# One scan and a long reciprocal per chunk, a shift in the weight merge, and a new order of the first 42 tasks, in a linear-attention and feed-forward kernel

## The chip, the cores and the metric

The kernel runs on one core of a Trainium2 chip. The metric is the device time of one execution in microseconds (us), the median of several runs; less is better. The engines are named as in the profile: PE is TensorE (matmuls), PEld its weight loads, DVE is VectorE, ACT is ScalarE, POOL is GpSimd, and SP is SyncE, which here only issues transfers (DMAs). Each engine works through its own list of instructions in order. SBUF is the working memory, PSUM the memory that PE writes to, in eight banks.

## The reference

The reference has two parts. The first is a linear attention over 768 positions for 4 batches and 8 heads of 48 dimensions, all in float32:

```python
for t in range(S):
    cur = einsum('bhd,bhe->bhde', u[None] * k_t, v_t)
    y[:, :, t] = einsum('bhd,bhde->bhe', r_t, state + cur)
    state = w_t[:, :, :, None] * state + einsum('bhd,bhe->bhde', k_t, v_t)
```

The decays w lie between 0.8 and 0.95. The second part takes the 3072 tokens of 384 values that come out of this: `h = x @ w_in` (384 to 2048), `g = h * sigmoid(1.702 h)`, `out = g @ w_out` (2048 to 384).

## The kernel before, in words

**Attention.** The positions are cut into chunks of 128; with 4 batches there are 24 chunks, six to a batch. Two heads share the partitions, so that a chunk is handled as four pairs of heads (NP = 4) on 112 partitions. For a chunk, DVE first makes running products of the decays with a scan along the free dimension, all four pairs in one instruction of 4 x 129 = 516 elements; a zero between the pairs starts each pair anew. Before, there are two scans: one backwards (line 288), which gives the products from each position to the end of the chunk (`li`) and at the pair's first place the product over the whole chunk (`total`); then a reciprocal of the four totals (line 291), which is written into the constant operand `d1f`; and a scan forwards that starts from it (line 293), giving `pm`. Then one multiplication (line 299) makes kq, that is k and r scaled by the two products. PE transposes kq (ps_t, 306), ACT copies the transposed half (kt, 308). The diagonal term with u comes from k times r (rku, 314), a small product on PE (ps_d, 326), a copy (s, 329) and a scaling of a masked identity by s (am): by eight ACT instructions for the chunks in `BY_ACT` (336), by two DVE instructions for the others (341). PE then makes the chunk's contribution to the state and the scores within the chunk (ps_u, 356 and 360). DVE multiplies the old state sf by `total` (366) and adds the contributions of the two halves (mid, 367, and the new sf, 370), and puts the scores into am (373). PE makes the output ps_y from am, v, qf, sf and mid (383, 396); a one-element copy (406) stands between two groups of these. At last `split` writes y as a high part in the format that PE takes (ACT, 230) and the rest as a low part (DVE, 231) into the tile x.

**Checks in the kernel.** The fast path is only right if no sum overflows. For this, ACT squares the tile of both products (`lp`) and kq and adds up (236); at the end a comparison over all these sums (571) decides whether a slow path is run.

**Feed-forward.** Weights arrive as 64-bit floats in 12 slices (`fetch`, tags f), six of w_in and six of w_out, through three buffers st. `convert` (tags w, four steps) turns a slice into a float32 and splits it: two ACT passes over the low and the high words (216, 217), two DVE merges (219, 222), the high part by ACT (224) and the low part by DVE (226). The tile x of a group of four chunks is 512 wide. A task is one of 16 column blocks of d_ff for one group; the first 20 tasks are half-width, each for two chunks of group 0. For a task PE makes ph (g, lines 438 to 440, nine matmuls), ACT makes gelu twice (h, 449 and 450), DVE the low part (gl, 452), and PE the second product po (y, 465 to 467, nine matmuls). Before the first product of a half group, a fill copies rows of x across partitions by six DMAs (425), of which SP and POOL issue three each.

**What sets the order.** For tasks from 42 on, a table of steps (`PARTS`) gives each piece of a chunk a place relative to its task. For the first 42 tasks the order is written out by hand in `RAMP`: each word is a piece (l a load, a the next step of a chunk, w of a weight slice, m of the sums, f, g, h, y, x as above, u and M small loads), and d with a number puts that many matmuls on constant data ahead of the next use of a PSUM bank. Every engine gets its instructions in this order.

Of the kernel before, what the change touches and what calls it, by code (L numbers as in the profile page):

```python
# [94 lines left out]
def rwkv_ffn_kernel(ctx: ExitStack, tc, wkr, vp, vrk, ub, w_in, w_out, masks, vt, uc, out):  # L95
# [133 lines left out]
    def split(hi, lo, f):  # L229
        A.copy(hi, f)  # L230
        V.tensor_tensor(lo, f, hi.bitcast(F32), op=ALU.subtract)
# [453 lines left out]
```

## Time and profile before

| What | Value |
|---|---|
| Median of 3 runs | 512.39 us (511.4 to 512.84) |
| Profiled execution | 512.25 us |
| Its span in the profile | 510.5 us |
| PE busy | 490.8 us, 5065 matmuls |
| DVE busy | 296.8 us, 507 instructions |
| ACT busy | 249.8 us, 532 instructions |
| DMA | 45.94 MB, mean 90 GB/s |

The span is the time between the first and the last instruction of the profiled execution. [...] In the rows of groups, the name left of the arrow is what is written and right of it what is read, then come shapes (partitions x elements) and count, then busy time in us, the mean of one in ns, and the idle time ahead of them with what ended it. In the rows of a timeline, the first number is the start and the second the length, in us.

### The profile page before, as it was taken

Reading aid. Unit: us, or ns where it says so; the run is one execution under the profiler, and the core shown is the slowest. Engines: PE = TensorE matmul, PEld = TensorE weight load, DVE = VectorE, ACT = ScalarE, POOL = GpSimd, SP = SyncE. Lnnn points to the kernel's source line nnn. Section 1 sums busy time; section 2 is a strip of 40 time slices with the busy share of each in tenths; the row PEclk is TensorE's granted clock in tenths of the full one; section 3 lists DMA queues with packets and bytes.
Section 4 is the critical chain, followed back from the end, with each engine's and each line's share of the span. In section 5 each row is a group of like instructions: output and inputs, shape, how many; then the busy total and the mean of one; then the engine's idle time right before and its main releaser. Section 6 shows DMA issues by size and latency. Waiting matters only on the chain.

```text
span 510.5 us, 11971 instructions
## 1 busy us (share of the span) xinstructions
PE 490.8 (96%) x5065; PEld 407.7 (80%) x5065; DVE 296.8 (58%) x507; ACT 249.8 (49%) x532; POOL 13.7 (3%) x45
## 2 busy tenths in 40 slices
PE   7788999999999999999999999999999999999994
PEld 3567999987888888888888888888888878888883
DVE  8899999787777762656556555555655521111110
ACT  4887989856726453352542543452552432322221
POOL 2010100000100010000001000001000000000000
PEclk9998899999999999999999999999999999999999
DMA  8988665034641532042204062204040001100001
GB/s 211 261 251 233 195 185 158 17 88 133 173 125 31 172 82 60 1 157 63 79 2 121 5 193 83 68 1 125 16 142 1 1 1 31 63 0 2 0 2 68
DMA packets 26830, 45.94 MB, mean 90 GB/s; under 512 B 4096, under 2 KB 17856, under 8 KB 26768
## 3 DMA queue, kind: packets, MB, share of 16 engines
q1 hardware_dynamic: 25984, 43.52, 29.9%
q0 software_dynamic: 672, 1.18, 1.2%
q8 instruction: 42, 0.69, 0.6%
q10 hardware_dynamic: 112, 0.39, 0.2%
q14 instruction: 20, 0.16, 0.1%
HBM read 38.00 MB, written 4.72 MB: 84 GB/s over the span
## 4 chain that ended last, share of the span: by engine, by line
PE 89%; DMA 5%; DVE 3%; ACT 1%; issue 1%; SPq 0%; DVEq 0%; ACTq 0%
PE po L465 14%; PE ph L438 13%; PE po L466 13%; PE po L467 13%; PE ph L439 13%; PE ph L440 13%; DMA wkr_t<-in_wkr 3%; PE ps_y L396 3%; PE ps_y L383 3%; PE ps_u L360 2%; PE ps_u L356 2%; DMA st<-in_w_in 2%; PE ps_t L306 2%; PE ps_d L326 1%; DVE lp L288 0%
## 5 line engine op out<-in xcount | busy, mean ns | idle before, releaser
L452 DVE TENSOR_TENSOR gl<-gf,gh 128x512 fp32r<-128x512 f32 (+1 forms) x106 | 67.9, 641 | 156.6 <-ACT gf L450 155.4
L449 ACT ACTIVATE gh<-ph 128x512 fp32r<-128x512 f32 (+1 forms) x106 | 59.2, 558 | 197.5 <-PE ph L440 177.8
L438 PE MATMUL ph<-x,wih 128*128 128x512 f32 (+1 forms) x318 | 119.8, 377 | 1.4 <-DMA x<-x 1.4
L465 PE MATMUL po<-gh,woh 128*128 128x512 f32 (+1 forms) x318 | 120.6, 379 | 0.0
L466 PE MATMUL po<-gh,wol 128*128 128x512 f32 (+1 forms) x318 | 118.2, 372 | 0.0
L467 PE MATMUL po<-gl,woh 128*128 128x512 f32 (+1 forms) x318 | 118.2, 372 | 0.0
L440 PE MATMUL ph<-x,wil 128*128 128x512 f32 (+1 forms) x318 | 117.4, 369 | 0.0
L439 PE MATMUL ph<-x,wih 128*128 128x512 f32 (+1 forms) x318 | 117.4, 369 | 0.0
L438 PEld LDWEIGHTS ph<-x,wih 128*128 128x128 f32 x318 | 59.9, 188 | 12.2 <-ACT junk L236 1.9
L465 PEld LDWEIGHTS po<-gh,woh 128*128 128x128 f32 x318 | 60.5, 190 | 10.8
L467 PEld LDWEIGHTS po<-gl,woh 128*128 128x128 f32 x318 | 60.6, 190 | 10.5 <-DVE gl L452 0.2
L466 PEld LDWEIGHTS po<-gh,wol 128*128 128x128 f32 x318 | 60.6, 191 | 9.5
L440 PEld LDWEIGHTS ph<-x,wil 128*128 128x128 f32 x318 | 59.9, 188 | 10.3
L439 PEld LDWEIGHTS ph<-x,wih 128*128 128x128 f32 x318 | 60.0, 189 | 9.4
L450 ACT ACTIVATE gf<-ph 128x512 f32<-128x512 f32 (+1 forms) x106 | 58.8, 555 | 2.7 <-DVE gl L452 2.6
L236 ACT ACTIVATE junk<-lp 112x1032 bf16<-112x1032 f32 x24 | 25.6, 1066 | 12.6 <-DVE lp L293 12.6
L299 DVE TENSOR_TENSOR kq<-wkr_t,lp 112x1024 f32<-112x1024 f32 x24 | 29.3, 1222 | 2.6 <-PE ps_y L396 1.6
L288 DVE TENSOR_TENSOR_SCAN lp<-wkr_t,d1r 112x516 f32<-112x516 f32 x24 | 29.4, 1225 | 1.7 <-DMA wkr_t<-in_wkr 1.7
L293 DVE TENSOR_TENSOR_SCAN lp<-wkr_t,d1f 112x516 f32<-112x516 f32 x24 | 29.6, 1231 | 0.7
L396 PE MATMUL ps_y<-kq,mid 64*64 64x64 f32 (+3 forms) x384 | 24.6, 223 | 3.6 <-DVE mid L406 1.4
L236 ACT ACTIVATE junk<-kq 112x1024 bf16<-112x1024 f32 x24 | 25.4, 1059 | 0.2
L396 PEld LDWEIGHTS ps_y<-kq,mid 64*64 64x64 f32 (+3 forms) x384 | 19.6, 130 | 5.6 <-DVE mid L406 2.1
(76 smaller groups left out, 475.1 us busy)
## 6 DMA issues: line engine op xcount, KB each, us to landing
st<-in_w_out SPq DMA_DIRECT2D x6, 1024.0 KB, 7.5
rk_t<-in_vrk SPq DMA_DIRECT2D x16, 384.0 KB, 3.5
st<-in_w_in SPq DMA_DIRECT2D x6, 896.0 KB, 8.4
v_t<-in_vrk SPq DMA_DIRECT2D x24, 192.0 KB, 2.8
out_t<-ob SPq DMA_DIRECT2D x18, 256.0 KB, 2.5
wkr_t<-in_wkr SPq DMA_DIRECT2D x18, 192.0 KB, 2.6
wkr_t<-in_wkr SPq DMA_DIRECT2D x36, 96.0 KB, 2.3
wkr_t<-in_wkr SPq DMA_DIRECT2D x5, 577.9 KB, 5.8
```

The lines of the kernel that those rows point to most:

```text
L236: A.activation(junk[:, 0 : x.shape[1]], x, AF.Square, accum_out=acc[0:R2, i : i + 1])
L293: V.tensor_tensor_scan(pm, w0, d1f.rearrange("r p c -> r (p c)"), 0.0, op0=ALU.mult, op1=ALU.add)
L396: T.matmul(ps[b][head(h), p], from_[head(half), p * D + OFF * h : p * D + HB], qf[head(half), p, blocks[b]], start=False, stop=p == PAIRS[ ...
L438: T.matmul(ph, h_, xs[i][:, 0, c, cs], start=c == 0, stop=False)
L439: T.matmul(ph, h_, xs[i][:, 1, c, cs], start=False, stop=False)
L440: T.matmul(ph, l_, xs[i][:, 0, c, cs], start=False, stop=c == NM - 1)
L449: A.activation(gh, ph, AF.Gelu_apprx_sigmoid, scale=1.0 / W_SCALE)
L450: A.activation(gf, ph, AF.Gelu_apprx_sigmoid, scale=1.0 / W_SCALE)
L452: V.tensor_tensor(gl, gf, gh.bitcast(F32), op=ALU.subtract)
L465: T.matmul(o, woh[:, f, ms], gh, start=first, stop=False, skip_group_check=True)
L466: T.matmul(o, wol[:, f, ms], gh, start=False, stop=False, skip_group_check=True)
L467: T.matmul(o, woh[:, f, ms], gl, start=False, stop=f == NF - 1, skip_group_check=True)
```

## The change

*One scan.* A chunk makes only the forward scan, which now starts from 1 in each pair (constant `begin`), so that pm holds the products from the chunk's start. `total` is pm's last element of each pair. The other factor, ip, is the reciprocal of all 516 elements of pm (line 290 of the new kernel). kq is made from both as before.

*State.* As k is now scaled by the inverse product from the start, the state is multiplied by `total` after the contributions are added and not before, once for each chunk but the last of a batch.

*Weights.* ACT writes the scaled low words, rounded to 16-bit integers, into the low halves of the high words. On DVE the first merge of two tiles is replaced by a shift of one tile by the constant 3, and one merge with a mask is left.

*Sums.* kq is no longer squared; the sum over lp stays. Instead the copies to x's high part add up their input (two accumulators a chunk), and at the end these sums are squared in one instruction.

*Who scales am.* For chunks 0 and 1 this is now done by DVE.

*Order.* `RAMP` is a new sequence, and one step of the sums is taken out of `PARTS`.

The start of DVE's list, from chunk 0's scan on. Before (288 and 293 are the scans, 291 the short reciprocal, wkr_t_82 belongs to chunk 0 and wkr_t_83 to chunk 1):

```order
L288 SCALAR_TENSOR_TENSOR lp<-wkr_t_82,d1r 112x516
L291 RECIPROCAL d1f<-lp 112x4
L293 SCALAR_TENSOR_TENSOR lp<-wkr_t_82,d1f 112x516
L299 TENSOR_TENSOR kq<-wkr_t_82,lp 112x1024
L314 TENSOR_TENSOR rku<-wkr_t_82 112x512
L288 SCALAR_TENSOR_TENSOR lp<-wkr_t_83,d1r 112x516
L291 RECIPROCAL d1f<-lp 112x4
L293 SCALAR_TENSOR_TENSOR lp<-wkr_t_83,d1f 112x516
L299 TENSOR_TENSOR kq<-wkr_t_83,lp 112x1024
L370 TENSOR_TENSOR sf_87<-ps_u_196,mid_90 112x192
```

The same place in the changed kernel (288 is the scan, 290 the long reciprocal, 297 kq, 311 rku, 338 the scaling of am, 366 and 367 the state, wkr_t_80 chunk 0 and wkr_t_81 chunk 1):

```order
L288 SCALAR_TENSOR_TENSOR lp<-wkr_t_80,begin 112x516
L290 RECIPROCAL lp<-lp 112x516
L297 TENSOR_TENSOR kq<-wkr_t_80,lp 112x1024
L311 TENSOR_TENSOR rku<-wkr_t_80 112x512
L338 TENSOR_TENSOR am<-same,s 128x256 x2
L366 TENSOR_TENSOR sf_85<-ps_u_182,mid_88 112x192
L367 TENSOR_TENSOR sf_85<-sf_85,lp 112x192
L370 COPY_PREDICATED am<-after,ps_u_181 128x256
L370 COPY_PREDICATED am<-after,ps_u_182 128x256
L288 SCALAR_TENSOR_TENSOR lp<-wkr_t_81,begin 112x516
```

Chunk 1's scan stood right behind chunk 0's rku; now chunk 0's am, state and scores come first.

SP's list around the first x fill (425, in the changed kernel 422). Before (200 and 202 fetch weight slices of w_in and w_out, 165 loads a chunk's w, k and r, 181 its v, 522 loads u):

```order
L200 DMA st<-in_w_in 16x2x1024
L522 DMA u_sb<-in_ub 128x384
L165 DMA wkr_t_83<-in_wkr 96x1541
L181 DMA v_t_84<-in_vrk 128x384
L165 DMA wkr_t_82<-in_wkr 96x1541
L425 DMA x<-x 16x2x256 x3
L202 DMA st<-in_w_out 128x2x1024
```

In the changed kernel (199 and 201 fetch slices, 164 loads a chunk):

```order
L199 DMA st<-in_w_in 16x2x1024
L201 DMA st<-in_w_out 128x2x1024
L422 DMA x<-x 16x2x256 x3
L164 DMA wkr_t_81<-in_wkr 96x1541
L199 DMA st<-in_w_in 112x2x1024
```

The second slice of w_out moved from behind the fill to ahead of it, and the load of chunk 3 (wkr_t_83 before, wkr_t_81 now) from ahead of the fill to behind it.

The diff, cut (of `RAMP` only its first row):

```diff
-BY_ACT = range(WHOLE)
+BY_ACT = (2,3,4,5,6,7)
...
-PARTS = [("a", -2, 2, 7), ("a", -1, 1, 7), ("a", 0, 1, 6), ("a", 1, 0, 5), ("m", 0, 2, 4), ("a", 1, 1, 4),
+PARTS = [("a", -2, 2, 7), ("a", -1, 1, 7), ("a", 0, 1, 6), ("a", 1, 0, 5), ("a", 1, 1, 4),
...
-l0 M l0 l0 l1 a0 a0 a0 m0 m0 d18 a0 f0 f1 l1 a0 a0 a0 a0 l2 l2 a1 a1 a1 a0 w0 m1 d4 a1 a1 d1 a1 a1 d9 a1 a0 a0 w0
+l0 l0 M l0 a0 l1 a0 a0 f0 m0 f1 d16 a0 a0 a0 a0 a0 a0 a0 w0 l1 a1 d5 a0 l2 l2 a1 a1 d7 a1 a1 a0 w0 a1 a1 f2 f3 a1
...
-    G.memset(d1r[:, :, C : C + 1], 1.0)
-    d1f = cp.tile([R2, NP, CW], F32, name="d1f")
-    G.memset(d1f, 0.0)
+    begin = cp.tile([R2, NP, CW], BF16, name="begin")
+    G.memset(begin, 0.0)
+    G.memset(begin[:, :, 0:1], 1.0)
...
+        h_low = st.bitcast(I16).rearrange("p k (n four) -> p (k n) four", four=4)[:, :, 2]
-        A.activation(l, l.bitcast(U32), AF.Copy, scale=L_SCALE)
         A.activation(cf, h.bitcast(F32), AF.Abs, scale=W_SHIFT, **sums)
+        A.activation(h_low, l.bitcast(U32), AF.Copy, scale=L_SCALE)
         yield
-        V.scalar_tensor_tensor(h, h, -(2 ** 31), l, op0=ALU.bitwise_and, op1=ALU.bitwise_or)
-        V.scalar_tensor_tensor(c, c, 3, h, op0=ALU.logical_shift_left, op1=ALU.bitwise_or)
+        V.tensor_single_scalar(c, c, 3, op=ALU.logical_shift_left)
+        V.scalar_tensor_tensor(c, h, 7 - 2 ** 31, c, op0=ALU.bitwise_and, op1=ALU.bitwise_or)
...
-    def split(hi, lo, f):
-        A.copy(hi, f)
+    def split(hi, lo, f, total=None):
+        A.activation(hi, f, AF.Copy, **({} if total is None else dict(accum_out=total)))
...
-        total = li.rearrange("r (p c) -> r p c", p=NP)[:, :, 0:1]
-        V.tensor_tensor_scan(
-            li[:, ::-1], w1[:, ::-1], d1r.rearrange("r p c -> r (p c)")[:, ::-1], 0.0, op0=ALU.mult, op1=ALU.add
-        )
-        V.reciprocal(d1f[:, :, 0:1], total)
-        yield
-        V.tensor_tensor_scan(pm, w0, d1f.rearrange("r p c -> r (p c)"), 0.0, op0=ALU.mult, op1=ALU.add)
+        total = pm.rearrange("r (p c) -> r p c", p=NP)[:, :, C : C + 1]
+        V.tensor_tensor_scan(pm, w0, begin.rearrange("r p c -> r (p c)"), 0.0, op0=ALU.mult, op1=ALU.add)
+        yield
+        V.reciprocal(ip, pm)
+        measures[t] = measured(t, lp)
         yield
...
-        measures[t] = measured(t, lp, kq.rearrange("r i p c -> r (i p c)"))
...
-            V.tensor_tensor(by_pair(sf), by_pair(sf), total.broadcast_to([R2, NP, D]), op=ALU.mult)
             V.tensor_tensor(by_pair(mid), us[0], by_pair(sf), op=ALU.add)
         if not final:
             new = state[t] = sfs[t % 3]
             V.tensor_tensor(by_pair(new), us[1], by_pair(mid), op=ALU.add)
+            V.tensor_tensor(by_pair(new), by_pair(new), total.broadcast_to([R2, NP, D]), op=ALU.mult)
...
-            split(x[0:R2, 0, :, cs], x[0:R2, 1, :, cs], ps[b][0:R2])
+            split(x[0:R2, 0, :, cs], x[0:R2, 1, :, cs], ps[b][0:R2], acc[0:R2, NT + 2 * t + b : NT + 2 * t + b + 1])
...
+    sums = acc[:, NT : 3 * NT]
+    V.tensor_tensor(sums, sums, sums, op=ALU.mult)
```

More of the change, by code (lines that the diff above doesn't have):

```diff
@@ L12 @@
 BF16 = mybir.dt.bfloat16
+I16 = mybir.dt.int16
 I32 = mybir.dt.int32
@@ L83 @@
-a11 a10 a9 a9 m10 a11 a11 y30 y31 y32 m11 l13 a11 a11 a10 a10 a11 a11 a11 a11 a11 g33 l12 a12 a12 m11 a12 g34 l13
-m12 a10 g35 g36 h33 h34 y33 y34 a12 m12 l14 a12 a13 a13 a11 a11 a13 l15 g37 a11 g38 g39 m13 m13 h35 y35 h36 h37 g40
-g41 h38 y36 h39 y37 h40 y38 y39 x11 h41
+l0 l0 M l0 a0 l1 a0 a0 f0 m0 f1 d16 a0 a0 a0 a0 a0 a0 a0 w0 l1 a1 d5 a0 l2 l2 a1 a1 d7 a1 a1 a0 w0 a1 a1 f2 f3 a1
+a1 a1 m1 w0 w0 d7 a1 a1 a2 a2 w1 a0 a1 x1 a2 m2 w1 w2 l3 w2 f4 w1 d13 a2 a2 l4 d3 g0 h0 g1 w2 l3 a2 w1 h1 a2 a2 y0
@@ L86 @@
+h41
 """
@@ L111, in rwkv_ffn_kernel @@
     G.memset(hm, 0.0)
-    d1r = cp.tile([R2, NP, CW], BF16, name="d1r")
-    G.memset(d1r, 0.0)
-    G.memset(d1r[:, :, C : C + 1], 1.0)
-    d1f = cp.tile([R2, NP, CW], F32, name="d1f")
-    G.memset(d1f, 0.0)
+    begin = cp.tile([R2, NP, CW], BF16, name="begin")
+    G.memset(begin, 0.0)
+    G.memset(begin[:, :, 0:1], 1.0)
     w_end = NP * CW + 1
@@ L149, in rwkv_ffn_kernel @@
     wih, wil, woh, wol = (cp.tile([P, NF, DM], F32R, name=x) for x in ("wih", "wil", "woh", "wol"))
-    acc = cp.tile([P, 2 * NT + 2 * NL], F32, name="acc")
+    acc = cp.tile([P, 3 * NT + 2 * NL], F32, name="acc")
     G.memset(acc, 0.0)
@@ L213, in convert @@
         l, h = w[:, :, 0], w[:, :, 1]
+        h_low = st.bitcast(I16).rearrange("p k (n four) -> p (k n) four", four=4)[:, :, 2]
         cf = c.bitcast(F32)
-        sums = {} if clamp else dict(accum_out=acc[:, 2 * NT + i : 2 * NT + i + 1])
-        A.activation(l, l.bitcast(U32), AF.Copy, scale=L_SCALE)
+        sums = {} if clamp else dict(accum_out=acc[:, 3 * NT + i : 3 * NT + i + 1])
         A.activation(cf, h.bitcast(F32), AF.Abs, scale=W_SHIFT, **sums)
+        A.activation(h_low, l.bitcast(U32), AF.Copy, scale=L_SCALE)
         yield
-        V.scalar_tensor_tensor(h, h, -(2 ** 31), l, op0=ALU.bitwise_and, op1=ALU.bitwise_or)
         if clamp:
             V.tensor_scalar(cf, cf, W_MAX, None, op0=ALU.min)
-        V.scalar_tensor_tensor(c, c, 3, h, op0=ALU.logical_shift_left, op1=ALU.bitwise_or)
+        V.tensor_single_scalar(c, c, 3, op=ALU.logical_shift_left)
+        V.scalar_tensor_tensor(c, h, 7 - 2 ** 31, c, op0=ALU.bitwise_and, op1=ALU.bitwise_or)
         yield
@@ L236, in measure, with measured @@
         A.activation(junk[:, 0 : x.shape[1]], x, AF.Square, accum_out=acc[0:R2, i : i + 1])
-    def measured(t, *xs):
-        for i, x in enumerate(xs):
-            measure(2 * t + i, x)
-            yield
+    def measured(t, x):
+        measure(t, x)
+        yield
     def head(h):
@@ L565, in rwkv_ffn_kernel @@
             do(token)
-    for x, limit in ((acc[:, 0 : 2 * NT], LIMIT), (acc[:, 2 * NT :], W_MAX)):
+    sums = acc[:, NT : 3 * NT]
+    V.tensor_tensor(sums, sums, sums, op=ALU.mult)
+    for x, limit in ((acc[:, 0 : 3 * NT], LIMIT), (acc[:, 3 * NT :], W_MAX)):
         V.tensor_single_scalar(x, x, limit, op=ALU.is_lt)
```

23 lines of the change are left out of this document (12 added, 11 removed).

## The prediction

> **What bounds the kernel now.** The page first: busy shares and the 40 slices of the span (12.8 us each).
>
> ```profile
> span 510.5 us, 11971 instructions
> PE 490.8 (96%) x5065; PEld 407.7 (80%) x5065; DVE 296.8 (58%) x507; ACT 249.8 (49%) x532; POOL 13.7 (3%) x45
> PE   7788999999999999999999999999999999999994
> DVE  8899999787777762656556555555655521111110
> PEclk9998899999999999999999999999999999999999
> ```
>
> TensorE (PE) is busy from the fifth slice to the end, VectorE (DVE) only in the first seven. So time saved on DVE or ScalarE (ACT) can count only near the start. How long the start lasts is told by the stretches for the tile po, the second product: after the stretch stand PE's busy time and, in brackets, its matmuls.
>
> ```profile
> 20.00:40.00 20.00, 1.45 (x10) 1.36 (x11) 0.00 (x0) 1.00 0.96 239
> 40.00:60.00 20.00, 6.38 (x36) 5.69 (x35) 0.00 (x0) 0.83 0.69 206
> 60.00:80.00 20.00, 10.28 (x81) 9.92 (x81) 0.00 (x0) 1.00 0.77 203
> ```
>
> All these matmuls are half-width, yet 36 fit into one 20 us and 81 into the next: until about 60 us PE is starved, behind that it is full. (Its granted clock of 0.83 in 40 to 60 explains a sixth of that, not a half.) What starves it is read from the engines in the same time; the columns are PE, weight loads, DVE, ACT, POOL, clock, DMA share, GB/s:
>
> ```profile
> 20.00:30.00 10.00, 8.09 (x163) 5.52 (x161) 9.00 (x15) 8.27 (x19) 1.07 (x2) 1.00 1.02 222
> 30.00:40.00 10.00, 8.31 (x109) 6.82 (x108) 9.72 (x15) 8.61 (x22) 0.56 (x2) 1.00 0.90 257
> 40.00:50.00 10.00, 7.80 (x154) 7.42 (x154) 9.54 (x14) 7.41 (x21) 0.00 (x0) 0.87 0.79 240
> 50.00:60.00 10.00, 9.99 (x72) 9.21 (x73) 9.04 (x13) 9.97 (x20) 1.49 (x3) 0.79 0.59 171
> ```
>
> DVE has 9.0 to 9.7 of every 10 us and works through its list without pause. I take it as what sets the pace up to 60 us, with ACT and the DMAs (0.9 to 1.0 until 40 us) close behind. So the change is counted as DVE's list up to the point where PE is full, then as what is left of it later.
>
> Four rows of DVE's timeline mark equal points of work in both orders: the first scan, the last x of chunk 1 (the first x fill and the first product hang on it), the gl of the ninth task, the last x of chunk 7.
>
> ```profile
> 5.15 1.23 DVE L288 TENSOR_TENSOR_SCAN lp<-wkr_t,d1r 112x516 f32<-112x516 f32 x1 [0.84 <-DMA wkr_t<-in_wkr]
> 27.87 0.75 DVE L231 TENSOR_TENSOR x<-ps_y,x 112x256 fp32r<-112x256 f32 x2
> 65.47 0.42 DVE L452 TENSOR_TENSOR gl<-gf,gh 128x256 fp32r<-128x256 f32 x1
> 126.28 1.43 DVE L231 TENSOR_TENSOR x<-ps_y,x 112x256 fp32r<-112x256 f32 x4
> ```
>
> So the points are 5.15, 28.62, 65.89 and 127.71 us.
>
> **The change, priced.** The groups of instructions, shapes kept apart (busy us, mean ns of one):
>
> ```profile
> L293 DVE TENSOR_TENSOR_SCAN lp<-wkr_t,d1f 112x516 f32<-112x516 f32 x24 | 29.6, 1231 | 0.7
> L299 DVE TENSOR_TENSOR kq<-wkr_t,lp 112x1024 f32<-112x1024 f32 x24 | 29.3, 1222 | 2.6 <-PE ps_y L396 1.6 <-DMA rk_t<-in_vrk 0.6
> L219 DVE SCALAR_TENSOR_TENSOR st<-st 128x1024 int32<-128x1024 int32 x12 | 14.6, 1218 | 1.3 <-ACT c L217 1.3
> L341 DVE TENSOR_TENSOR am<-same,s 128x256 f32<-128x256 f32 x32 | 12.1, 418 | 0.2
> L319 DVE TENSOR_REDUCE s<-rk_t 128x8 f32<-128x384 f32 x16 | 8.8, 553 | 0.6
> L226 DVE TENSOR_TENSOR wol<-c,woh 128x1024 fp32r<-128x1024 f32 x6 | 7.3, 1220 | 1.3 <-ACT woh L224 1.3
> L366 DVE TENSOR_TENSOR sf<-sf,lp 112x192 f32<-112x192 f32 x20 | 7.0, 350 | 0.0
> L314 DVE TENSOR_TENSOR rku<-wkr_t 112x512 f32<-112x512 f32 x8 | 5.5, 684 | 0.0
> L291 DVE RECIPROCAL d1f<-lp 112x4 f32<-112x4 f32 x24 | 4.4, 182 | 0.8
> L406 DVE COPY mid<-ps_y 1x1 f32<-1x1 f32 x16 | 2.3, 146 | 25.1 <-PE ps_y L396 25.1
> L573 DVE TENSOR_REDUCE oks<-acc 128x1 f32<-128x60 f32 x1 | 0.2, 203 | 0.0
> L571 DVE TENSOR_SCALAR acc<-acc 128x48 f32<-128x48 f32 x1 | 0.2, 179 | 0.0
> L571 DVE TENSOR_SCALAR acc<-acc 128x12 f32<-128x12 f32 x1 | 0.2, 164 | 0.0
> ```
>
> Two prices are not in the trace. *The shift S* (one source, 1024 elements): L571 grows from 164 to 179 ns over 36 elements, 0.42 ns each, so 0.164 + 1012 x 0.42 ns = 0.59 us; at the other end it costs what L219 costs, 1.22. I take 0.59, from the only rows with one source and a constant.
>
> *The long reciprocal R* (516 elements) decides the case. Four elements cost 182 ns. If what is over in that row is a fixed fee and the elements stream like those of the reduction (203 to 553 ns over 324, 1.08 ns each), R = 0.182 + 512 x 1.08 ns = 0.74 us. If the excess belongs to the elements, it depends on the fixed part: L571's line meets zero elements at 159 ns, which leaves 23 ns, 5.75 each, R = 3.1 us; the line through L366 and L299 (1.05 ns each) meets it at 149, which leaves 8.25 each, R = 4.4 us; the reduction's line at 138 would leave 11 each, R = 5.8. No other row of DVE needs over 150 ns or so before its elements count, so I give the excess to the elements and take **R = 3.4 us**, near L571, the row nearest in size.
>
> [...]
>
> *First stretch* (to 28.62). Against before, DVE's list has 3 scans fewer (-3.68), 3 short reciprocals fewer (-0.55), one kq (-1.22) and one rku (-0.68) fewer, one two-source merge fewer (-1.22); 4 am multiplications for chunks 0 and 1 more (+1.67), 2 one-element copies more (+0.29), one state multiplication more (+0.35), one shift and 3 long reciprocals: -5.04 + S + 3R = -4.45 + 3R. Waits stay alike: before there were these two,
>
> ```profile
> 16.46 1.23 DVE L219 SCALAR_TENSOR_TENSOR st<-st 128x1024 int32<-128x1024 int32 x1 [1.28 <-ACT c L217]
> 21.00 1.23 DVE L288 TENSOR_TENSOR_SCAN lp<-wkr_t,d1r 112x516 f32<-112x516 f32 x1 [0.83 <-DMA wkr_t<-in_wkr]
> 9.78 1.05 PE L326 MATMUL ps_d<-hm,rku 112*128 112x2 f32 x8
> 10.87 0.17 ACT L329 COPY s<-ps_d 128x8 f32<-128x8 f32 x1
> ```
>
> 2.1 us together. Now chunk 1's scan no longer stands ahead of chunk 0's am, and DVE waits behind rku for ps_d and s, 1.05 + 0.17 and two hand-overs, 1.3 us, then some 0.5 for the copy of mid: 1.8.
>
> *Second stretch* (to 65.89): 2 scans fewer (-2.46), 2 short reciprocals (-0.36), 6 merges become shifts (6 x -0.63 = -3.78), one low half of weights fewer (-1.22), one rku more (+0.68), 2R: -7.14 + 2R.
>
> Together **-11.6 + 5R**: zero at R = 2.3, +5.4 at 3.4. As PE is starved here, it moves with this.
>
> *Third stretch* (to 127.71): 4 scans (-4.92), 4 short reciprocals (-0.73), 5 shifts (-3.15), one kq and one low half more (+2.44): -6.36 + 4R = +7.2 at 3.4. PE is full here, and DVE has room:
>
> ```profile
> sum 70.00, PE 68.76 PEld 62.97 DVE 59.50 ACT 54.89 POOL 1.50; mean PE 9.82 PEld 9.00 DVE 8.50 ACT 7.84 POOL 0.21
> ```
>
> That is the sum over 60 to 130 us: 10.5 us idle, 2.6 a chunk, against 3.4 - 1.41 = 2.0 more a chunk. It mostly fits; half of one reciprocal's surplus, 1.0, I leave uncovered, since a gl queued behind a reciprocal comes 3.4 us later and ACT's next gelu and PE's second product wait for it.
>
> *At no cost:* after 130 us DVE's share is 5 to 7 tenths and the 2.0 a chunk lie under PE; with that cover gone they would be 16 x 2.0 = 32 us. Two groups of ACT and the DMA row of the chunk loads:
>
> ```profile
> L236 ACT ACTIVATE junk<-kq 112x1024 bf16<-112x1024 f32 x24 | 25.4, 1059 | 0.2
> L236 ACT ACTIVATION_READ_ACCUMULATOR junk<-kq 112x1 f32 x24 | 4.7, 198 | 0.0
> wkr_t<-in_wkr SPq DMA_DIRECT2D x5, 577.9 KB, 5.8
> ```
>
> ACT loses this sum of squares (1.06 + 0.20 us a chunk) for two accumulator reads (0.20 each), and the am of two chunks; with DVE's list longer by 5.4 us ACT is the earlier of the two, so this earns nothing at R = 3.4. On SP's queue the second w_out slice moves ahead of the first x fill, and chunk 3's load behind it; that load takes 5.8 us, and between the fill and chunk 3's scan DVE has some 10 us of work (kq, two shifts and merges, two low halves), so it is hidden. The multiplication of all accumulators runs where L571 ran, 100 us before the end.
>
> Sum: 5.4 + 1.0 = +6.4 on the profiled execution's 512.25 us (span 510.5 and 1.75 around it; the median of the runs is 512.39): **518.7**.
>
> **Rivals.**
> *Faster: the reciprocal streams.* R = 0.74 gives -7.9 up to the ninth gl and -3.4 in the third stretch, where PE is full and nothing follows. ACT is relieved alike. The DMAs, at 0.9 to 1.0 until 40 us, speak against the full sum; I take -6: 506.3. It decides below R = 2.3. Against it: the 182 ns.
> *Much slower: 8.25 ns an element.* R = 4.4 gives +10.4, then +11.2 against 10.5 us of room, of which I leave 2.5 uncovered: 525.
> *Between.* R near 2 gives -1.6 up to the ninth gl: 511, hardly told from 512.
> *The other end of S*, 1.22, would add 7 x 0.63 = 4.4 to any of them.
>
> **Chances.** Forecast (R 3 to 3.9) 0.45, much slower 0.13, streaming 0.33, between 0.09, of which faster, same and slower get a third each. A difference under 0.3% (1.5 us) can't be told from none. Faster 0.36, same 0.04, slower 0.60. The likeliest case's own range is 515 to 523; as streaming holds a third, the range has to reach it: 505 to 526.
>
> **What will show it.** The row of the long reciprocal: above 2.3 us the kernel is slower, below it faster; everything else is second to it. Chunk 1's x should end near 34 us (near 26 if it streams) and the ninth gl near 71 (near 59); DVE's busy time should grow by 24 x 2.0 - 12 x 0.63 + 1.7 = 42 us. The shift's row should be 0.6. PE should stand longer before chunk 0's transposes, which wait for kq. I am wrong if R is long and the ninth gl still comes no later, as then DVE did not set the pace, or if PE has gaps after 130 us.

## The result, and the profile after

The changed kernel takes **555.98 us** (median of 4 runs, 555.68 to 558.14) against 512.38 (511.4 to 512.84): ratio 1.0863, 95% interval 1.0831 to 1.0895. It is slower, as forecast, but by 43.6 us and not by 6.4.

The page of the changed kernel: span, busy times, and the slices of PE, DVE and PE's granted clock (13.9 us each).

```profile
span 554.4 us, 11928 instructions
PE 512.2 (92%) x5068; PEld 414.2 (75%) x5068; DVE 337.9 (61%) x490; ACT 242.6 (44%) x514; POOL 14.2 (3%) x44
PE   6777988879799889999999999999999999999993
DVE  6789787596898968546757656675766612111110
PEclk8788899988999999999999999999999999999997
```

PE is full only from the sixteenth slice (about 208 us), and DVE is heavily used as long as that. The stretches of the tile po, the second product (PE's busy time and matmuls first, PE's clock third from the end), and then those of all engines (PE, weight loads, DVE, ACT, POOL, clock, DMA share, GB/s):

```profile
20.00:40.00 20.00, 0.00 (x0) 0.00 (x0) 0.00 (x0) 0.91 0.30 86
40.00:60.00 20.00, 2.42 (x18) 2.21 (x18) 0.00 (x0) 0.76 0.76 197
60.00:80.00 20.00, 6.02 (x46) 5.75 (x47) 0.00 (x0) 0.98 0.39 114
```

```profile
20.00:30.00 10.00, 6.83 (x94) 4.71 (x93) 8.71 (x11) 3.51 (x6) 0.00 (x0) 0.83 0.41 104
30.00:40.00 10.00, 6.33 (x87) 3.57 (x86) 9.66 (x13) 7.16 (x16) 1.46 (x2) 1.00 0.18 68
40.00:50.00 10.00, 10.00 (x123) 9.05 (x121) 9.06 (x14) 9.61 (x20) 0.56 (x2) 0.83 0.92 219
50.00:60.00 10.00, 6.48 (x114) 5.80 (x116) 8.14 (x8) 8.20 (x16) 0.00 (x0) 0.70 0.59 174
...
160.00:200.00 40.00, 35.88 (x451) 27.99 (x450) 34.51 (x50) 14.79 (x33) 0.09 (x1) 1.00 0.40 114
```

Where 36 and 81 matmuls of po stood in 40 to 60 and 60 to 80 us there are 18 and 46, and even in 160 to 200 us PE lacks 4.1 us, where it lacked 0.8 in the kernel before:

```profile
160.00:200.00 40.00, 39.18 (x374) 32.30 (x365) 24.89 (x45) 18.26 (x38) 1.50 (x3) 1.00 0.38 101
```

The groups that the change touches (busy us, mean ns of one, idle time ahead and who ended it):

```profile
L290 DVE RECIPROCAL lp<-lp 112x516 f32<-112x516 f32 x24 | 81.0, 3376 | 0.7
L221 DVE TENSOR_SCALAR c<-c 128x1024 int32<-128x1024 int32 x12 | 8.3, 688 | 1.2 <-ACT c L216 1.0
L217 ACT ACTIVATE st<-st 128x1024 int16<-128x1024 uint32 x12 | 30.5, 2543 | 0.4
L222 DVE SCALAR_TENSOR_TENSOR c<-st,c 128x1024 int32<-128x1024 int32 x12 | 14.7, 1228 | 9.8 <-ACT st L217 9.4
```

The reciprocal (3.38 us) and the shift (0.69) cost about what was taken. L217 has no price in the prediction: ACT's pass to int16 takes 2.54 us where the pass to int32 took 1.17 (it is the row L216 of the kernel with the old merge, quoted under experiment 2), and DVE's 12 merges wait 9.4 us for it in all.

The marks of equal work, in DVE's timeline: first scan, last x of chunk 1, ninth gl, last x of chunk 7.

```profile
5.31 1.23 DVE L288 TENSOR_TENSOR_SCAN lp<-wkr_t,begin 112x516 f32<-112x516 f32 x1 [1.00 <-DMA wkr_t<-in_wkr]
36.88 1.35 DVE L231 TENSOR_TENSOR x<-ps_y,x 112x256 fp32r<-112x256 f32 x4
80.95 0.42 DVE L449 TENSOR_TENSOR gl<-gf,gh 128x256 fp32r<-128x256 f32 x1 [0.18 <-ACT gf L447]
156.89 1.41 DVE L231 TENSOR_TENSOR x<-ps_y,x 112x256 fp32r<-112x256 f32 x4
```

They end at 38.23, 81.37 and 158.30 us: 9.6, 15.5 and 30.6 later than before. I follow this lag below by the end of the k-th gl (of 106), read the same way in every run's timeline of DVE and set against the kernel before:

| us later than before, at gl | 9th (65.9) | 31st (155.7) | 43rd (211.0) | last (498.6) |
|---|---|---|---|---|
| changed kernel | 15.5 | 31.5 | 34.9 | 42.0 |
| b9, division alone | 10.9 | 17.5 | 22.6 | 22.9 |
| b2, merge alone | 7.7 | 10.4 | 10.5 | 10.5 |
| b3, place in SBUF alone | 3.9 | 3.7 | 4.9 | 11.9 |
| b7, sums alone | 0.4 | -0.1 | -0.1 | -0.1 |
| e7, sequence and sums | 3.0 | 5.3 | 5.2 | 5.5 |
| e5, all but the sequence | 25.5 | 33.2 | 39.0 | 46.1 |

In brackets: when that gl ends in the kernel before. The start differs by some us from one execution to the next, with PE's clock there: b3 computes the same as the kernel before, but was granted 0.53 in 10 to 20 us where that had 1.00, and is 3.9 us late at the ninth gl. So differences of 4 us that arise there are not read; what grows later is.

### The profile page after: what moved, and what is told of

It reads as the page before. It is cut to its first block, busy times and chain, and to the rows that moved or that the text cites. A ratio compares the mean times of both kernels' runs of the same rounds, so it can differ in the third digit from the quotient of the medians.

```text
span 554.4 us, 11928 instructions
## 1 busy us (share of the span) xinstructions
PE 512.2 (92%) x5068; PEld 414.2 (75%) x5068; DVE 337.9 (61%) x490; ACT 242.6 (44%) x514; POOL 14.2 (3%) x44
## 4 chain that ended last, share of the span: by engine, by line
PE 64%; DVE 7%; issue 0%; ACT 0%; DVEq 0%
PE po L462 10%; PE po L464 10%; PE po L463 10%; PE ph L435 9%; PE ph L437 9%; PE ph L436 9%; DVE lp L290 3%; PE ps_y L380 2%; PE ps_u L357 1%; PE ps_y L393 1%; PE ps_t L303 1%; PE ps_u L353 1%; DVE kq L297 1%; DVE lp L288 1%; DVE gl L449 0%; DVE x L231 0%
## 5 line engine op out<-in xcount | busy, mean ns | idle before, releaser
L464 PE MATMUL po<-gl,woh 128*128 128x512 f32 (+1 forms) x318 | 120.5, 379 | 5.6 <-DVE gl L449 5.5
L435 PE MATMUL ph<-x,wih 128*128 128x512 f32 (+1 forms) x318 | 122.1, 384 | 1.5 <-ACT gf L447 1.4
L462 PE MATMUL po<-gh,woh 128*128 128x512 f32 (+1 forms) x318 | 122.0, 384 | 0.6 <-ACT gh L446 0.6
L437 PE MATMUL ph<-x,wil 128*128 128x512 f32 (+1 forms) x318 | 120.1, 378 | 0.0
L436 PE MATMUL ph<-x,wih 128*128 128x512 f32 (+1 forms) x318 | 119.5, 376 | 0.0
L290 DVE RECIPROCAL lp<-lp 112x516 f32<-112x516 f32 x24 | 81.0, 3376 | 0.7
L437 PEld LDWEIGHTS ph<-x,wil 128*128 128x128 f32 x318 | 60.6, 191 | 11.9
L447 ACT ACTIVATE gf<-ph 128x512 f32<-128x512 f32 (+1 forms) x106 | 58.8, 555 | 11.9 <-DVE gl L449 11.9
L303 PE MATMUL ps_t<-ident,kq 112*128 112x112 f32 (+1 forms) x96 | 14.3, 273 | 20.7 <-DVE kq L297 20.7
L217 ACT ACTIVATE st<-st 128x1024 int16<-128x1024 uint32 x12 | 30.5, 2543 | 0.4
L303 PEld LDWEIGHTS ps_t<-ident,kq 112*128 112x128 f32 (+1 forms) x96 | 10.8, 141 | 26.1 <-DVE kq L297 13.5
L288 DVE TENSOR_TENSOR_SCAN lp<-wkr_t,begin 112x516 f32<-112x516 f32 x24 | 29.4, 1226 | 1.3 <-DMA wkr_t<-in_wkr 1.0
```

The source lines that it names most:

```text
L288: V.tensor_tensor_scan(pm, w0, begin.rearrange("r p c -> r (p c)"), 0.0, op0=ALU.mult, op1=ALU.add)
L290: V.reciprocal(ip, pm)
L435: T.matmul(ph, h_, xs[i][:, 0, c, cs], start=c == 0, stop=False)
L436: T.matmul(ph, h_, xs[i][:, 1, c, cs], start=False, stop=False)
L437: T.matmul(ph, l_, xs[i][:, 0, c, cs], start=False, stop=c == NM - 1)
L447: A.activation(gf, ph, AF.Gelu_apprx_sigmoid, scale=1.0 / W_SCALE)
```

## The experiments

Times are medians; the ratio, with its 95% interval, is to the kernel before run beside it (511.3 to 512.7).

**1. The division.** e1 puts the two scans back into the changed kernel; b1 and b9 put the one scan and the long reciprocal into the kernel before. Core of the edit in b1 (reversed in e1):

```diff
-        V.tensor_tensor_scan(li[:, ::-1], w1[:, ::-1], ...)
-        V.reciprocal(d1f[:, :, 0:1], total)
-        V.tensor_tensor_scan(pm, w0, d1f..., ...)
+        V.tensor_tensor_scan(pm, w0, begin..., ...)
+        tot = at.tile([R2, NP, 1], F32, tag="tot", name="tot", bufs=3)
+        V.tensor_copy(tot, total)
+        V.reciprocal(ip, pm)
```

> The changed kernel, 556.0 us, with only the division put back as it was: two scans and a reciprocal of 4 elements a chunk in place of one scan and the reciprocal of 112x516 (3.38 us), the state multiplied before the new part is added. (24 small copies of the total into a tile of its own are added on VectorE, because the buffer with the product has no room to wait.) Theory 'the division': the reciprocal costs VectorE 2.1 us a chunk more than the second scan did, and stands in the chain scan, reciprocal, keys, transposes that the trace shows at 152 to 206 us; the ninth gl comes 8 to 10 us earlier than 80.95, and the time falls to 535 to 542. Rival 'the conversion pass': ScalarE's int16 write (2.54 us where the int32 write took 1.17) paces the weights, and the division lies beside it; the time stays above 550. Rival 'the new sequence of the tasks': the same, above 550, because the sequence itself makes TensorE wait.

Measured: e1 531.6, 1.0388 (1.0329 to 1.0447), 24.4 us less than the changed kernel, more than expected.

> The kernel before, in its own sequence, with only the division changed: one scan, the reciprocal of 112x516 and the state multiplied after the sum (the total copied to a tile of its own, 12 small copies more). Putting the two scans back into the changed kernel took 24 us off. Theory 'the division costs this in any sequence': VectorE gets 2.1 us a chunk more while it is at 9 to 9.7 of 10 us, and the chain of a chunk grows by as much; 530 to 538. Rival 'the division is dear only in the new sequence, which puts the transposes right behind it': in the sequence before, other tasks stand between, and the time stays under 521 (512 and the 2.1 us of the first four chunks). Rival of the prediction (its own sum): about 518.7.

Measured: b1 540.71, 1.0554 (1.0523 to 1.0584), above both rivals and a little above the theory. The tile `tot` had moved x of the odd groups in SBUF; b9 is b1 with a spacer that undoes this:

```diff
+    at.tile([P, 40], F32, name="pad3")
```

> The kernel before with only the division changed, as in the earlier run of that edit (540.7), with an unused tile that brings x of the odd groups back to the place it had (the small tile for the total had moved it by 96 bytes). Theory 'the place of x in the odd groups was a quarter of the slow matmuls': 2 to 3 us less, 537 to 539, and the lag of the gl behind the kernel before stands still from 211 us on, at 23 to 25. Rival 'the division also costs the steady state': 540 to 542, the lag growing as before.

Measured: b9 536.55, 1.0483 (1.0451 to 1.0516), 4.2 us less than b1 and just under the theory. So the division alone costs 24.3 us in the old sequence as well (with its copy of the total, 0.17 us a chunk, on 24 chunks), and the lag stands still from the 43rd gl on: all of it arises before 200 us. Where? Sums over 60 to 180 us, of the kernel before and of b9:

```profile
sum 120.00, PE 117.93 PEld 103.38 DVE 98.53 ACT 79.35 POOL 1.50; mean PE 19.66 PEld 17.23 DVE 16.42 ACT 13.23 POOL 0.25
```

```profile
sum 120.00, PE 112.92 PEld 98.09 DVE 106.28 ACT 80.65 POOL 3.00; mean PE 18.82 PEld 16.35 DVE 17.71 ACT 13.44 POOL 0.50
```

In b9 DVE still has 13.7 us idle of 21.5 before, and PE lacks 7.1 us, 5.0 more than before. DVE's idle time took up only a part. The chain of waits of the changed kernel suggests why, from one chunk's state to the next (start, us):

```profile
162.86 0.37 DVE sf L367
163.31 1.24 DVE lp L288
164.58 3.39 DVE lp L290
167.99 1.24 DVE kq L297
169.37 0.57 PE ps_t L303 x4
...
174.16 0.62 PE ps_y L380 x31
...
175.24 0.67 DVE am L338 x2
175.91 0.60 DVE gl L449
176.51 0.28 DVE mid L363
...
177.28 0.37 DVE sf L367
177.67 1.24 DVE lp L288
178.93 3.38 DVE lp L290
```

Scan, reciprocal and kq stand behind each other ahead of the transposes, and the next chunk's scan stands on DVE's list behind this chunk's am and state, which wait for PE. This chunk so goes once round a loop of 14.4 us (163.31 to 177.67), and the reciprocal lies in it in full. In the old sequence the loss comes chunk by chunk as well. The first scans of the seventh and of the fourteenth chunk, before and in b9:

```profile
102.18 1.22 DVE L288 TENSOR_TENSOR_SCAN lp<-wkr_t,d1r 112x516 f32<-112x516 f32 x1
180.50 1.22 DVE L288 TENSOR_TENSOR_SCAN lp<-wkr_t,d1r 112x516 f32<-112x516 f32 x1
```

```profile
113.65 1.22 DVE L288 TENSOR_TENSOR_SCAN lp<-wkr_t,begin 112x516 f32<-112x516 f32 x1
202.18 1.23 DVE L288 TENSOR_TENSOR_SCAN lp<-wkr_t,begin 112x516 f32<-112x516 f32 x1
```

They are 11.5 and 21.7 us late: 10.2 us more over seven chunks, 1.5 a chunk, where the division adds 2.1 (3.38 - 1.41 and the copy). From the fifteenth chunk on the lag stays at 22.6. DVE's idle time does not lie free in between. In 60 to 180 us, before and in b9, most of it is gl waiting for ACT's gelu (us in total, times, longest):

```profile
DVE gl L452 <- ACT gf L450: 11.9, 13, 3.2
```

```profile
DVE gl L451 <- ACT gf L449: 7.1, 9, 1.8
```

In the chain above such a gl stands between a chunk's am and its state, inside the loop. That the loop is the whole cause in b9 is argued from this, as no run leaves the loop alone and lengthens DVE's list elsewhere.

**2. The merge.** e2 puts the old merge back into the changed kernel, b2 the new one into the kernel before (shown as in b2):

```diff
-        A.activation(l, l.bitcast(U32), AF.Copy, scale=L_SCALE)
         A.activation(cf, h.bitcast(F32), AF.Abs, scale=W_SHIFT, **sums)
+        A.activation(h_low, l.bitcast(U32), AF.Copy, scale=L_SCALE)
-        V.scalar_tensor_tensor(h, h, -(2 ** 31), l, op0=ALU.bitwise_and, op1=ALU.bitwise_or)
-        V.scalar_tensor_tensor(c, c, 3, h, op0=ALU.logical_shift_left, op1=ALU.bitwise_or)
+        V.tensor_single_scalar(c, c, 3, op=ALU.logical_shift_left)
+        V.scalar_tensor_tensor(c, h, 7 - 2 ** 31, c, op0=ALU.bitwise_and, op1=ALU.bitwise_or)
```

> The changed kernel with only the merge of the weights put back: ScalarE converts to int32 (1.17 us a piece before, 2.54 us now) and VectorE merges in two steps. Theory 'the conversion pass': ScalarE loses 1.37 us on each of 12 pieces, 16.4 us in all, and the 9.4 us that VectorE waits for st go; the time falls to 538 to 545. Rival 'the division': VectorE, not ScalarE, sets the pace of the first 170 us, and gets 0.54 us more a piece to do; the time stays within 3 us of 556. Rival 'the new sequence': within 3 us of 556 as well.

Measured: e2 554.27, 1.0814 (1.0767 to 1.0862): 1.7 us less than the changed kernel, as the rivals had it.

> The kernel before with only the merge of the weights changed: ScalarE writes int16 (2.54 us a piece instead of 1.17), VectorE shifts by a constant and merges once. ScalarE gets 16.4 us more within the first 110 us, VectorE loses 0.54 us on each of 12 pieces. Theory 'ScalarE's pass is a bottleneck of the first stretch': ScalarE is at 8.3 to 9 of 10 us from 10 to 100 us, so a good half of the 16.4 us shows; 518 to 526. Rival 'VectorE alone bounds the first stretch': the 6.4 us that VectorE saves show, and the time falls to 506 to 511. In the changed kernel the old merge took off 1.7 us alone and 5.2 us with the division put back; if it is the same here, 514 to 517.

Measured: b2 522.26, 1.0192 (1.0171 to 1.0212). Alone it costs 9.5 us, and all of that by the 31st gl; with the two scans put back it is worth 5.2 us (e1 against e3, below), and beside the division it is mostly hidden (e2), presumably since DVE is then the later of the two. That it is ACT's pass and not the merge is told by two more runs and a measuring piece. b10 gives ACT one more pass (13.9 us in all) and leaves the merge alone; b11 has the new merge, with the int16 written densely into a scratch tile, so that the low bits are missing from the weights.

```diff
 b10
+        A.activation(cf, l.bitcast(U32), AF.Copy, scale=L_SCALE)
         A.activation(cf, h.bitcast(F32), AF.Abs, scale=W_SHIFT, **sums)
 b11, against b2
-        A.activation(h_low, l.bitcast(U32), AF.Copy, scale=L_SCALE)
+        low = (pool if clamp else at).tile([R2, 2 * NP * CW], BF16, tag="junk", name="junk")[:, 0:n].bitcast(I16)
+        A.activation(low, l[0:R2].bitcast(U32), AF.Copy, scale=L_SCALE)
```

> The kernel before with its old merge, and one more pass of ScalarE over each of the 12 pieces: it writes l to c as int32 (1.1 us) just before the pass that overwrites c. VectorE's work and the result are unchanged. This gives ScalarE 13 us more, where the int16 write gave it 16. Theory 'it was ScalarE's longer pass that made the new merge 10 us slower': the time goes up by 7 to 10, to 519 to 522. Rival 'it was the shape of the merge (VectorE waits for the later of the two passes, the shift comes first)': under 515.

> The kernel before with the new merge, but ScalarE's int16 goes dense into a scratch tile and not into every fourth half-word of st: 1.09 us by the measuring run where the strided write took 2.46 there. The low bits are so left out of the weights: this is for the time alone. VectorE still saves 0.54 us a piece. Theory 'the stride of the two-byte write was the whole loss': the 10 us go, and VectorE's 6.4 us less show at least in part; 506 to 511. Rival 'the new merge loses by itself': 515 or more. If VectorE's saving is worth nothing: 511.5 to 513.

Measured: b10 520.29, 1.0162 (1.014 to 1.0185); b11 513.7, 1.002 (0.9999 to 1.004). ACT's work alone makes a loss of that size, and without the strided write the new merge is no faster than the old: the 0.54 us a piece that DVE saves are worth nothing that can be told. b10's two rows of ACT and the merge, for comparison with L217 and L222 above:

```profile
L216 ACT ACTIVATE st<-st 128x1024 int32<-128x1024 uint32 x12 | 14.1, 1174 | 0.0
L220 DVE SCALAR_TENSOR_TENSOR st<-st 128x1024 int32<-128x1024 int32 x12 | 14.7, 1222 | 4.1 <-ACT c L218 4.1
```

The measuring piece, behind the end of the kernel before, on idle engines:

> The kernel before with a measuring piece behind its end (its time is not of interest): four times each, on otherwise idle engines, ScalarE's pass over 128x1024 from uint32 at every 8th byte to int32 at every 8th byte (as before: 1.17 us), int32 dense, int16 at every 8th byte (as changed: 2.54 us), int16 at every 4th, int16 dense, the last also from a dense source, and the same from f32 to f32 and bf16; on VectorE the reciprocal of 112x258, 112x516 and 112x1032 and a multiply of 112x516. Theory 'the type int16 is dear': all three int16 forms 2.5 us, bf16 near 1.1. Rival 'writing two bytes at a stride is dear': int16 dense near 1.1, int16 and bf16 at a stride 2.5. Rival 'it was the contention of the full kernel': int16 at every 8th byte under 1.5 here. Reciprocal: if it goes by the element, 1.7, 3.4 and 6.7 us; with a fixed part, less than double from one to the next.

Each row is one form; `by` stands for a stride of 8 bytes (of the int16 forms 8 and 4 bytes together), `src` is read at every 8th byte, `den` densely:

```profile
L599 ACT ACTIVATE i_by<-src 128x1024 int16<-128x1024 uint32 x8 | 14.4, 1926 | 0.0
L602 ACT ACTIVATE b_by<-src 128x1024 bf16<-128x1024 f32 x4 | 9.8, 2460 | 0.0
L602 ACT ACTIVATE b_dense<-src 128x1024 bf16<-128x1024 f32 x4 | 4.6, 1139 | 0.0
L599 ACT ACTIVATE i_by<-src 128x1024 int32<-128x1024 uint32 x4 | 4.4, 1106 | 6.1 <-DVE src L583 6.1
L599 ACT ACTIVATE i_dense<-src 128x1024 int16<-128x1024 uint32 x4 | 4.4, 1094 | 0.0
...
L605 DVE RECIPROCAL quot<-num 112x1032 f32<-112x1032 f32 x4 | 26.4, 6603 | 0.1
L604 DVE RECIPROCAL quot<-num 112x516 f32<-112x516 f32 x4 | 13.5, 3378 | 0.1
L603 DVE RECIPROCAL quot<-num 112x258 f32<-112x258 f32 x4 | 7.1, 1766 | 0.1
```

The int16 row mixes two forms; the first record of the one at 8 bytes, from ACT's timeline, tells them apart:

```profile
512.06 2.46 ACT L599 ACTIVATE i_by<-src 128x1024 int16<-128x1024 uint32 x1
```

So int16 takes 2.46 us at 8 bytes and, from the mean of 1.93, 1.39 at 4. It is not the type or the stride by itself: int16 dense takes 1.09 us, int32 at 8 bytes 1.11. A two-byte result written at a stride of 8 bytes is dear, bf16 (2.46) as well as int16. The reciprocal goes by the element: (6.603 - 1.766) / 774 = 6.25 ns.

**3. Both put back.** e3 is e1 and e2 together.

> The changed kernel with both the division and the merge put back, so that of the change only the new sequence of the first 42 tasks, the one sum of squares a chunk and the sums taken with ScalarE's split are left. Theory 'division and conversion pass together': 520 to 528, what remains being the pace of TensorE's tail (233 where it was 227 ns a matmul, some 8 to 11 us). Rival 'the new sequence of the tasks': the sequence was written for other durations and makes TensorE wait by itself; 535 or more.

Measured: e3 526.43, 1.0281 (1.0237 to 1.0325), at the upper end of the theory. 29.5 of the 43.6 us are gone; 14.1 above the kernel before are left, more than the 8 to 11 that the tail was to explain. Its places in SBUF are still unlike (see 4) and its sequence is the new one (see 5).

**4. The place in SBUF.** In the changed kernel the lag grows on by 7 us behind the 43rd gl, though PE waits for nothing there (busy 189.72 of 190 us from 300 to 490, as before). The change drops the constant `d1f` (2064 bytes a partition) and lengthens `acc` by 96 bytes. So wih, wil, woh and wol begin at 20224 and so on, where it was 22304 (they lie a multiple of 256 apart), and x, gh and gl at 118880 and so on, where it was 120864. By remainders of 256, weights and activations were both at 32 and are now at 0 and 96. Spacers move them with nothing computed differently:

```diff
 e4 (changed kernel, 32 and 32)
+    cp.tile([R2, NP, CW], F32, name="pad2")
+    cp.tile([P, 40], F32, name="pad1")
 b3 (kernel before, 64 and 96); b4 has pad0 alone: 64 and 64; b8 has pad1 alone, with 64 bytes: 32 and 96
+    cp.tile([P, 8], F32, name="pad0")
     wih, wil, woh, wol = ...
     acc = ...
+    cp.tile([P, 8], F32, name="pad1")
```

> The changed kernel with two unused tiles between its own, so that the weights and the activations lie in SBUF at the same remainder of 64 bytes (32) as in the kernel before; in the changed kernel the weights lie at remainder 0. Nothing is computed differently. Theory 'the place in SBUF sets the matmul's pace': the tail falls back from 4.20 to 4.08 us a task of 18 matmuls, and the time by 8 to 11 us, to 545 to 548. Rival 'the chip's clock or its power state sets it': no change, 554 to 558, and the tail still at 4.20.

> The kernel before, nothing computed differently, with two unused 32-byte tiles that put the weights at remainder 0 of 64 bytes and leave the activations at 32, as in the changed kernel. Moving the changed kernel to 32 and 32 made its matmuls of 512 columns 389 to 390 ns where 394 to 397 stood. Theory 'the place in SBUF': the tail slows from 4.08 to 4.20 us a task of 18 matmuls, and the time goes up by 4 to 8 us, to 516 to 520. Rival 'the later and lower clock of the changed kernel left the pace': no change, 511 to 513.5.

> The kernel before with one unused 32-byte tile, so that weights and activations both lie at remainder 0 of 64 bytes. Theory 'weights and activations have to lie alike': pace and time as before, 511 to 513.5. Theory 'what counts is the remainder of the weights, 32 being the better': 516 to 520, as with weights alone at 0. Theory 'rows that begin at a multiple of 64 are read faster': under 510.

Measured: e4 550.95, 1.0744 (1.0694 to 1.0794), 5.0 us less; b3 522.42, 1.0184 (1.0136 to 1.0233); b4 511.82, 0.9983 (0.9968 to 0.9997). So in these runs neither remainder matters by itself: both alike gave the time of the kernel before (b4), unlike ones 9.7 us more (b3). e4's theory of 8 to 11 us was too large: its lag no longer grows behind the 43rd gl (37.4 there and at the last, where the changed kernel has 34.9 and 42.0), but its profiled run had already lost 2.5 us more by then. I had counted in remainders of 64. b6, written for the sums (experiment 5), had 32 and 160, alike to 64 but not to 256, and was slow; b8 asks for 64:

> The kernel before, nothing computed differently, with an unused 64-byte tile behind acc: weights at remainder 32 of 256, activations at 96. Differences of 32, 96, 128 and 192 have been slow so far, 0 fast. Theory 'only a difference of 0 to 256 is fast': TensorE's tail at 4.20 us a task, 518 to 522. Rival 'a multiple of 64 is enough': 511 to 513.

Measured: b8 514.85, 1.0056 (1.0034 to 1.0078), between the two. The same group of matmuls from 300 to 490 us, in the order before, b3, b4, b6, b8:

```profile
L440 PE MATMUL ph<-x,wil 128*128 128x512 f32 x126 | 49.0, 389 | 0.0
```

```profile
L442 PE MATMUL ph<-x,wil 128*128 128x512 f32 x123 | 48.6, 395 | 0.0
```

```profile
L441 PE MATMUL ph<-x,wil 128*128 128x512 f32 x126 | 49.1, 390 | 0.0
```

```profile
L441 PE MATMUL ph<-x,wil 128*128 128x512 f32 x125 | 49.3, 395 | 0.0
```

```profile
L441 PE MATMUL ph<-x,wil 128*128 128x512 f32 x126 | 49.4, 392 | 0.0
```

(A matmul's recorded duration overlaps the next: at 321 us in the kernel before they start 0.23 us apart, with 0.39 recorded for each. At the end of the kernels, where nothing else runs on PE, the gl come every 4.08 us before and every 4.20 us after, for 18 matmuls: 227 and 233 ns each.) The mean distance of the gl from the 57th to the 105th, with the chunks' matmuls in it:

| Activations less weights, mod 256 | Runs | us from gl to gl |
|---|---|---|
| 0 | before, b4, b7, e4 | 4.51, 4.51, 4.51, 4.48 |
| 64 | b8 | 4.54 |
| 32 | b3 | 4.62 |
| 96 | changed kernel | 4.60 |
| 128 | b6 | 4.60 |

All in stretches with a granted clock of 1.00. Some 0.1 us on each of the 63 tasks behind the 43rd gl is the 7 us by which b3 and the changed kernel fall back there; with 1.0 from the ninth to the 43rd, b3's trace gives the place 8.0 us. Its median has 9.7, but its runs lie in two pairs (520.1 and 520.5, 524.3 and 524.7), and the profiled one, of the upper pair, was 3.9 late at the start.

**5. The sequence and the sums.** b6 and b7 put only the sums into the kernel before (b7 with the spacer at 160 bytes, which keeps 32 and 32); e6 and e7 are the changed kernel with the division, the merge and the place put back (in e6 x of the odd groups was still 128 off); e5 is the changed kernel with the old sequence. Who scales am in chunks 0 and 1 stays as in the changed kernel in e5 to e7.

```diff
 b6, b7
-        measures[t] = measured(t, lp, kq.rearrange("r i p c -> r (i p c)"))
+        measures[t] = measured(t, lp)
-            split(x[0:R2, 0, :, cs], x[0:R2, 1, :, cs], ps[b][0:R2])
+            split(x[0:R2, 0, :, cs], x[0:R2, 1, :, cs], ps[b][0:R2], acc[0:R2, NT + 2 * t + b : NT + 2 * t + b + 1])
```

> The kernel before in its own sequence with only the sums changed: the square pass over kq (0.97 us on ScalarE) goes, and the sum of x is taken by the two ScalarE splits that are there already (a read of the accumulator, 0.2 us each, follows every one). ScalarE saves about 0.6 us a chunk, some 5 us by 140 us, and there it is at 8.3 to 9 of 10 us. Theory 'ScalarE's list is part of the first stretch's bound': 1 to 4 us faster, 508 to 511. Rival 'VectorE alone bounds it': no change, 511 to 513.5. Slower, if the read of the accumulator stands between a split and the next: 514 to 516.

> The kernel before with only the sums changed, as in the earlier run of that edit (520.4), but with the unused tile behind acc at 160 bytes instead of 32, so that the activations lie at 120992 + 128 = 121120, a multiple of 256 from the weights as in the kernel before, and not 128 off. In the earlier run the gl came 1 to 2 us sooner than before up to 190 us, and from 200 us on each task took 0.11 us longer. Theory 'the place counts to 256 bytes': the late growth goes, and the time is 509.5 to 511.5 against about 512. Rival 'the sums taken by the splits slow the steady state': 519 or more again. If the read of the accumulator costs the steady state only a little: 512 to 515.

Measured: b6 520.35, 1.0177 (1.0097 to 1.0257), outside every case written down, by the place; b7 512.95, 1.0021 (1.0 to 1.0043). b7 is above its theory (509.5 to 511.5), in the case that was put third. The late growth is gone, and the sums alone change nothing that can be told, though ACT's busy time falls by 20 us (249.8 to 229.9).

> The changed kernel with division, merge and places in SBUF (all at remainder 32) as before, so that the new sequence, the one sum of squares and the sums taken with ScalarE's split are left. With the places as in the changed kernel it took 526.4. Theory 'the place was 8 to 10 of those 15': 516 to 519, TensorE's tail at 4.08 us a task, and a lag of 4 to 7 us behind the kernel before that stands since about 170 us and no longer grows. Rival 'the place costs only when the operations are new': no change, 525 to 527.

> The changed kernel with division, merge and places in SBUF as before, as in the earlier run (520.6), in which x of the odd groups was still 128 bytes off. Theory: 2 us less, 517 to 519; the lag stands still at about 5 us from 211 us on, and is what the new sequence costs when the operations are the old ones. Rival 'the sums cost the steady state': 520 to 521.5.

Measured: e6 520.59, 1.017 (1.01 to 1.024), just outside the theory, by that x (e7 is 2.3 lower); e7 518.28, 1.0114 (1.0085 to 1.0144), within it, its lag still at 5.2 to 5.5 us. With the old operations the new sequence loses about 6 us, by the 31st gl (the 24 small copies of the total, 0.14 us each, are a part of it, at most 1.7 us by then).

> The changed kernel with the sequence of tasks of the kernel before (its table of the first 42 tasks and its steady rules), every other part of the change kept, and its places in SBUF (weights at remainder 0 of 64, activations at 32). 12 small copies of the total are added. From the kernel before the parts alone cost 28.0 (division), 9.5 (merge), 9.7 (place), 47.2 in all against 43.6 for the whole change. Theory 'the parts add up and the new sequence is worth little': 555 to 562. Rival 'the new sequence loses time by itself' (the changed kernel with both operations put back stood 15 above the kernel before, of which the place explains 8 to 10): under 551. Rival 'the new sequence is what makes the new operations bearable': over 565.

Measured: e5 558.43, 1.0893 (1.0816 to 1.097). With the new operations the old sequence is no better than the new: 2.4 us more in the medians, 4 in the lag, within the intervals.

**The account.** From the kernel before, one part at a time: division 24.3, merge 9.5, place 9.7 (8.0 by the trace), new sequence 6.0 with the sums, which alone are worth nothing. They add up to 49.5 and not to the 43.6 of the whole, so they overlap; that the first three come to 43.5 is chance. Taken away from the changed kernel, the same parts give 24.4, 1.7 and 5.0, and the sequence -2.4: there the merge hides behind the division, and the sequence costs nothing. No version tried beats the kernel before; b4 and b7 equal it.

## Why the prediction was right or wrong

- *The prices.* R = 3.4 (measured 3.38) was right and S = 0.59 (0.69) near, and DVE's busy time grew by 41.1 us (42 forecast). The excess of the four-element row did belong to the elements (6.25 ns each in p1); that R came out within 0.02 is in part luck, as the rows allowed 3.1 to 5.8.
- *First and second stretch, -11.6 + 5R.* For the division the count holds: 5 chunks at 3.38 - 1.41 are 9.9, and b9 is 10.9 late at the ninth gl, as far as the start can be read. For the merge the sign was wrong: counted as 7 x 0.63 = 4.4 saved, it was 7.7 late in b2. The step that failed here is the one on ACT, "this earns nothing": the diff's other half, the pass that now writes 16-bit integers, was given no price of its own, though it has another output type. It costs 1.37 us more on each of 12 pieces, 16.4 in all.
- *"I take it as what sets the pace up to 60 us."* Half true. Lengthening DVE's list costs all of it up to the ninth gl (b9), but a longer ACT list costs more than half of it too (b10: 8 us late for 13.9 added), and shortening DVE's gains nothing (b11). Both engines bound the start. The rivals that had the kernel faster rested on DVE alone, and b11 suggests that the gain would have been small.
- *Third stretch, "it mostly fits": +1.0.* This is the largest error, and the step is the overlap: idle time of DVE was counted as room for the reciprocal. From the ninth gl to the 43rd b9 falls back by another 11.7 us, 6.6 of them up to the 31st (155.7 us), although DVE had 10.5 us of idle time in 60 to 130. About half of that time was spent in waiting for gelu in the middle of a chunk's round (5.5 us), and each round became 1.5 us longer. The order of the list hinted at it: scan to kq precede the transposes in every chunk. I had named the price with the cover gone (7.2), and most of the cover was gone.
- *"At no cost" after 130 us.* For the division right only later: b9's lag grows by 5.1 us from the 31st gl (155.7 us) to the 43rd (211.0) and stands still from there. That ACT's dropped sum of squares earns nothing was right as well (b7). But the sign "PE has gaps after 130 us" did come: PE lacks 4.1 us in 160 to 200 us.
- *What no term covered:* 5 us (e4) to 7 us (the lag) in the changed kernel from PE's pace, by tiles that only moved, and the sequence, which I priced by the count of what it moves.
- *Small slips.* The pieces named between the x fill and chunk 3's scan add up to 7.3 us, not to "some 10"; the load was covered all the same, as all 24 scans together waited 1.0 us for loads. The chances of the cases add up to 0.61 for slower and 0.03 for same.
- *The signs.* Chunk 1's x at 38.2 (34 forecast) and the ninth gl at 81 (71) told early that the sum was too small. The wait ahead of chunk 0's transposes came: 4.13 us, where it was 1.48, in PE's timelines of the changed kernel and of the one before:

```profile
11.37 0.98 PE L303 MATMUL ps_t<-ident,kq 112*128 112x112 f32 x4 [4.13 <-DVE kq L297]
```

```profile
9.27 0.57 PE L306 MATMUL ps_t<-ident,kq 112*128 112x112 f32 x4 [1.48 <-DVE kq L299]
```

What stays open: how much of the 24 us of the division is the lower clock of the start (0.83 in b9's first 60 us, where the kernel before had 0.94, and 0.51 to 0.83 at places in the changed kernel) was not tried apart. Why the place of two tiles against each other sets PE's pace is not known either, only that in these runs it does (4.08 and 4.20 us a task at the end).

## What to carry to other kernels

Do not count an engine's idle time as room before asking what it waits for there and whether the new work stands in the same round: follow one round of the chain, from a chunk's state to the next one's, before calling a longer instruction covered. Price every instruction whose output type or stride changes (here ACT's pass to int16, 2.54 us for 1.17), on the other engine too, and not only those that the change is about. After any edit that adds, drops or resizes a tile, compare the matmul's mean duration in the steady state; if it moved by a per cent (here from 389 to 395 ns in b3), look at the addresses before looking for a cause in the work.
